# A new band build, loads of w in thirds, mixed first blocks and a SyncE store at the end of a fused convolution and maxout FFN

**Chip, cores, metric.** One core of one Trainium2 chip. The metric is the device time of one execution in microseconds (us), lower is better. Most kernels were run in several rounds beside the kernel before on the same chip. Each trace is one of those runs.

## The reference

A causal convolution with 7 softmaxed taps for each of 8 heads (24 channels each) over x of 8 x 4160 x 192, then a maxout feed-forward layer over the 33280 rows. All inputs and outputs are fp32.

```python
w = softmax(weight)                                  # 8 heads x 7 taps
y[b, s, h, :] = sum_k w[h, k] * x_pad[b, s + k, h, :]   # 6 zero rows ahead
h = max(max(y @ w1, y @ w2), y @ w3)                 # 192 -> 768
out = h @ w_out                                      # 768 -> 192
```

## The kernel before

The rows are cut into 65 blocks of 512. Each block passes through: load of x (SyncE), cast to fp16 (GpSimd), convolution as matmuls with a banded matrix of taps (`conv`, tile G), eviction to `ys`, a *repack* of `ys` into `yd` by six small DMAs (three on SyncE, three on GpSimd), a *doubling* of `yd` onto partitions 64 to 127 (one DMA on SyncE), layer 1 in six steps (`l1`, tiles lp and lq), and the second stage (`st2`, tile po). Blocks 0 and 1 are convolved in another way (`conv_dense`, tile D), with no repack. `wd` holds w1-w3 and w2-w3; `keep_warm` runs matmuls on zeros in places where TensorE would wait.

The band before: the taps are spread over 128 partitions by an fp32 matmul, softmaxed there, multiplied into seven shifted identities on VectorE and summed by seven matmuls.

```python
nc.tensor.matmul(wps, lhsT=ones[:], rhs=wk[:], start=True, stop=True)
# ... exp, sums, reciprocal, taps ...
for k in range(KW):                       # 7 products on VectorE
    nc.vector.tensor_mul(out=shifted[:, k, :, :], in0=shifted_identity_k, in1=taps_k)
keep_warm(7)
for k in range(KW):                       # 7 matmuls
    nc.tensor.matmul(ps[:], lhsT=ident16[:], rhs=shifted[:, k, :, :], start=(k == 0), stop=(k == KW - 1))
```

The order of the loads and of the first blocks, shortened:

```python
load_x(0); load_w(...)          # 6 pieces of w on SyncE and ScalarE
load_x(1); load(wos)
for t in range(2, 6): load_x(t) # x of blocks 2 to 5, all in the first burst
# ...
conv_dense(0, ...); l1(0, 0); l1(0, 1); l1(0, 2); l1(0, 3); transposes
conv_dense(1, ...); conv(2); l1(0, 4); repack(2); load_x(6); make_m(0); l1(0, 5); make_m(1)
conv(3); repack(3); double(2); load_x(7)
for t in range(1, NB):
    load_x(t + 7); cast_x(t + 5); double(t + 2)
    l1(t, 0); conv(...); repack(t + 3); st2(t - 1, ...); l1(t, 1..5)
    store(t - 1, 0, 4, (nc.gpsimd,))       # also for the last block but one
```

The softmax here doesn't subtract the row's maximum and nothing guards it: scores larger than these inputs give would overflow.

## Time and profile before

| | before |
|---|---|
| time | 482.04 us median (481.05 to 482.09, 3 runs) |
| span of the profiled core, mean granted TensorE clock | 480.0 us, 0.993 |
| TensorE busy | 468.4 us, 98% of the span |
| loop | 13.95 us for two blocks, all TensorE |

The prediction below shows the lines of this profile. One more view of it matters later: what TensorE waited for between 14 and 60 us (columns: who, for whom, us in total, times, longest). "issue" is idle time that no semaphore explains.

```profile
PE pt L284 <- DVE h L388: 1.3, 2, 1.1
PE pm L301 <- issue: 0.2, 1, 0.2
```

So from 14 us on TensorE lost 1.5 us in all. The 0.2 us of "issue" ahead of make_m (tile pm) looked like nothing.

Words used below: a DMA *lands* when its completion is signalled. A *stop* is idle time of TensorE that the profile calls "issue". A *window* is a stretch of 3.41 us: the granted clock is 1.00 or 0.50 in these traces from about 8 us on, and up to the last matmul it changed only after multiples of it (10.24 us at 1.00, then 3.41 at 0.50 before). A *pass* is one turn of the loop over t.

### The profile page before, as it was taken

The page shows a single profiled execution, that of the slowest core. Times are in us where ns is not written, and L with a number is a line of the kernel's source. Part 1 is how long each engine was busy: PE and PEld are TensorE (multiplying, and loading weights), DVE is VectorE, ACT ScalarE, POOL GpSimd, SP SyncE. Part 2 cuts the span into 40 slices and gives each one's busy share as a digit, 9 for nine tenths or more (in the row PEclk, how much of TensorE's full clock was granted, in tenths as well). Part 3 has the DMA queues.
Part 4 walks back from the last instruction along what each step waited for, and adds up shares of the span by engine and source line. Part 5 has one row for each costly group of instructions (what it writes and reads, how often), then busy time and mean ns, then how long its engine had stood idle before and what let it go on. Part 6 is the DMA issues. An engine that isn't in the chain of part 4 may idle for free.

```text
span 480.0 us, 21944 instructions
## 1 busy us (share of the span) xinstructions
PE 468.4 (98%) x9083; PEld 393.7 (82%) x9083; DVE 365.8 (76%) x609; ACT 327.1 (68%) x608; POOL 211.3 (44%) x341
## 2 busy tenths in 40 slices
PE   7899999999999999999999999999999999999994
PEld 3578888888888888888888888888888888888994
DVE  6667877778777877877787787778777777778774
ACT  5676667676666767666666766676676767667663
POOL 2654534553454355445435544543545354345210
PEclk9899999999999999999999999999999999999998
DMA  8877756665766665566666657566556666644312
GB/s 198 216 188 209 214 147 194 173 187 160 202 168 181 184 184 165 162 196 179 173 179 185 171 155 196 168 189 178 170 158 191 186 169 176 179 126 135 112 44 95
DMA packets 67603, 82.08 MB, mean 171 GB/s; under 512 B 9424, under 2 KB 55760, under 8 KB 67504
## 3 DMA queue, kind: packets, MB, share of 16 engines
q1 hardware_dynamic: 53934, 49.01, 40.6%
q0 software_dynamic: 13216, 31.38, 18.4%
q8 instruction: 71, 1.16, 1.1%
q10 hardware_dynamic: 354, 0.30, 0.2%
q14 instruction: 28, 0.23, 0.1%
HBM read 30.31 MB, written 25.56 MB: 116 GB/s over the span
## 4 chain that ended last, share of the span: by engine, by line
PE 96%; ACT 1%; DVE 1%; issue 0%; POOL 0%; POOLq 0%
PE lp L383 32%; PE po L426 30%; PE lq L383 26%; PE G L322 7%; PE D L342 1%; PE idle L196 1%; ACT r L387 0%; PE band_sum L245 0%; ACT band L268 0%; ACT w3h L262 0%; DVE h L388 0%; DVE xz L216 0%; PE pm L305 0%; PE wps L223 0%; DVE band L218 0%
## 5 line engine op out<-in xcount | busy, mean ns | idle before, releaser
L388 DVE TENSOR_TENSOR h<-r,lq 128x512 f16<-128x512 f16 x390 | 266.9, 685 | 101.8 <-ACT r L387 101.8
L387 ACT ACTIVATE r<-lp 128x512 f16<-128x512 f32 x390 | 232.7, 597 | 135.0 <-PE lp L383 89.8
L383 PE MATMUL lp<-yd,wd 64*128 64x512 f16 x1170 | 315.4, 376 | 0.1
L383 PE MATMUL lq<-yd,wd 64*128 64x512 f16 x1170 | 314.6, 375 | 0.0
L426 PE MATMUL po<-wo,h 64*128 64x192 f16 x3120 | 231.3, 243 | 0.1
L426 PEld LDWEIGHTS <-h 64*128 64x128 f16 x3120 | 186.9, 94 | 26.1 <-issue 0.3
L383 PEld LDWEIGHTS <-wd 64*128 64x128 f16 x2340 | 164.4, 94 | 20.9 <-issue 1.4
L452 POOL DMA_DIRECT2D out_dram<-o x64 | 50.7, 792 | 245.9 <-DVE o L436 229.1
L366 POOL DMA_DIRECT2D yd<-ys x189 | 95.5, 509 | 2.2 <-ACT ys L353 1.4
L426 PE MATMUL po<-m,yd 64*128 64x192 f16 x780 | 86.8, 243 | 0.0
L436 DVE TENSOR_TENSOR o<-a,po 128x384 f32<-128x384 f32 (+1 forms) x132 | 71.3, 541 | 0.6 <-ACT a L435 0.6
L146 POOL CAST x<-xf 112x960 f16<-112x960 f32 x62 | 61.6, 995 | 2.3 <-DMA xf<-in_x_dram 2.3
L435 ACT COPY a<-po 128x384 f32<-128x384 f32 (+1 forms) x132 | 61.8, 469 | 1.2 <-PE po L426 1.2
L426 PEld LDWEIGHTS <-yd 64*128 64x128 f16 x780 | 55.0, 94 | 8.1
L322 PEld LDWEIGHTS <-x 112*32 112x32 f16 x2480 | 30.0, 97 | 13.3 <-issue 13.1
L353 DVE CAST ys<-G 128x512 f16<-128x512 f32 x60 | 38.4, 681 | 0.0
L353 ACT CAST ys<-G 128x512 f16<-128x512 f32 x66 | 35.8, 589 | 2.2 <-PE G L322 0.9
L322 PE MATMUL G<-band,x 112*32 112x103 f16 (+1 forms) x2480 | 35.0, 210 | 0.0
L161 POOL CAST xz<-xf 112x240 f16<-112x240 f32 (+2 forms) x6 | 2.4, 450 | 11.3 <-DMA xf<-in_x_dram 11.3
L196 PE MATMUL idle<-idle 128*128 128x512 f16 x14 | 5.7, 546 | 1.2 <-DVE unit L212 1.2
L342 PE MATMUL D<-band,xz 112*32 112x103 f16 (+1 forms) x240 | 4.1, 240 | 1.0 <-ACT band L268 1.0
L342 PEld LDWEIGHTS <-xz 112*32 112x32 f16 x240 | 3.8, 114 | 1.5 <-issue 1.4
(50 smaller groups left out, 41.2 us busy)
## 6 DMA issues: line engine op xcount, KB each, us to landing
out_dram<-o POOLq DMA_DIRECT2D x64, 384.0 KB, 3.9
xf<-in_x_dram SPq DMA_DIRECT2D x57, 420.0 KB, 4.8
yd<-yd SPq DMA_DIRECT2D x63, 192.0 KB, 3.2
yd<-ys SPq DMA_DIRECT2D x63, 48.0 KB, 3.6
yd<-ys POOLq DMA_DIRECT2D x63, 48.0 KB, 3.3
xf<-in_x_dram SPq DMA_DIRECT2D x8, 252.0 KB, 3.1
yd<-ys SPq DMA_DIRECT2D x63, 32.0 KB, 3.2
yd<-ys POOLq DMA_DIRECT2D x63, 32.0 KB, 2.9
```

The costliest lines, as they stand in the source:

```text
L146: nc.gpsimd.tensor_copy(out=v[0:rl, q0:q1, :], in_=xf[0:rl, q0:q1, :])
L322: nc.tensor.matmul(G[i][32 * g:32 * g + 32, lo:hi], lhsT=x16[0:rlen, cb:cb + 32], rhs=band[0:rlen, h, cc:cc + hi - lo], start=True, stop=T ...
L342: nc.tensor.matmul(ps[32 * g:32 * g + 32, lo:hi], lhsT=xz[t][0:rlen, q, v, 32 * s:32 * s + 32], rhs=band[0:rlen, h, cc:cc + hi - lo], star ...
L353: copy(out=slots[t][:, i, :], in_=convs[t][i][:])
L366: (nc.sync, nc.gpsimd)[n % 2].dma_start(out=yd[r0:r0 + rows, c, :], in_=slots[t][s0:s0 + rows, half, :])
L383: nc.tensor.matmul(ps[i][:, 0:N], lhsT=wd[row, c, P * j:P * (j + 1)], rhs=y[row, c, 0:N], start=(c == 0), stop=(c == NC - 1))
L387: nc.scalar.activation(out=r[:, 0:N], in_=ps[0][:, 0:N], func=AF.Relu)
L388: nc.vector.tensor_max(out=hs[t][:, j, 0:N], in0=r[:, 0:N], in1=ps[1][:, 0:N])
L426: nc.tensor.matmul(ps[b0, i][:, s % 2, :], lhsT=a, rhs=b, start=first, stop=last)
L435: nc.scalar.copy(out=a[:, ss, :], in_=ps[s0, 0][:, ss, :])
L436: nc.vector.tensor_add(out=outs[t][:, s0:s + 1, :], in0=a[:, ss, :], in1=ps[s0, 1][:, ss, :])
L452: qs[i].dma_start(out=bass.AP(tensor=out.tensor, offset=r * D, ap=[[D, n], [step * D, s1 - s0], [1, D]]), in_=ob[p0:p0 + n, s0:s1, :])
```

## The change

The intent is to reach the loop earlier and to end sooner. The band comes from a zero-padded line of taps, of which 38 tiny matmuls each take a window. w comes in thirds on SyncE with x of block 1 between. Layer-1 steps of blocks 0 and 1 are mixed, so that TensorE has work while w and x arrive. The last block but one is stored by SyncE, so that no GpSimd store stands at the end. Cut to its core:

```diff
-    for t in range(2, 6):
+    load_x(0); load_w(0); load_w(1); load_x(1); load_w(2)
+    for t in range(2, 5):
         load_x(t)
...
-    (taps matmul, 7 products, 7 matmuls)
+    nc.vector.tensor_scalar(out=line[:, 31:31 + KW], in0=wexp[:], scalar1=wrec[:], scalar2=None, op0=mult)
+    for c in range(WIN):                                       # 38
+        nc.tensor.matmul(bps[:, c, :], lhsT=line[:, WIN - 1 - c:WIN + 31 - c],
+                         rhs=ident16[0:NHEAD, 0:NHEAD], start=True, stop=True)
+    keep_warm(6)
...
+    nc.gpsimd.dma_start(out=wo[:], in_=moe_w_out...)           # fp32 to fp16 in the DMA
+    l1(0, 0); make_wd(2, 4); transposes; l1(0, 1); l1(0, 2); l1(0, 3)
+    conv_dense(1, ...); make_wd(4, 6); l1(1, 0); l1(0, 4); transposes; l1(0, 5); l1(1, 1)
+    conv(2); l1(1, 2); repack(2); make_m(0); make_m(1); st2(0, ...); l1(1, 3); ...
+    load_x(5); double(2); load_x(6); l1(1, 4); ...; l1(1, 5)
+    conv(3); repack(3); cast_x(4); cast_x(5); cast_x(6); load_x(7); load_x(8)
...
+    convs_at = {2: (4, 5), 3: (6,)}
+    repacks_at = {2: (4,), 3: (5, 6)}
+    doubles_at = {2: (3,), 3: (4,), 4: (5, 6)}
-    for t in range(1, NB):
+    for t in range(2, NB):
         load_x(t + 7)                                          # stands ahead of double(u)
         cast_x(t + 5)
-        double(u - 1)
+        for u in doubles_at.get(t, (t + 2,)):
+            double(u)
...
-        store(t - 1, 0, 4, (nc.gpsimd,))
+        (last block but one: two halves on nc.sync; the others as before)
```

More of the change, by code (lines that the diff above doesn't have):

```diff
@@ L97 @@
     psw = ctx.enter_context(tc.tile_pool(name="psw", bufs=4, space=bass.MemoryType.PSUM))
-    NDENSE, AHEAD = 2, 3
+    NDENSE = 2
     SLOTS = ((0, 1, 2, 3), (6, 7, 4, 5))
@@ L109, with load_x @@
     x16z = const.tile([P, nlast * D + 2 * EDGE], FP16, name="x16_z")
-    def load_x(t):
+    def load_x(t, eng=nc.sync):
         if not 0 <= t < NB:
@@ L129, in load_x @@
                           ap=[[D, rlen], [step * D, k - i + 1], [1, D]])
-            nc.sync.dma_start(out=xf[0:rlen, i:k + 1, :], in_=src)
+            eng.dma_start(out=xf[0:rlen, i:k + 1, :], in_=src)
             if parts and parts[-1][0] == rlen:
@@ L156, in cast_dense @@
         for v, copy in enumerate(copies):
+            if copy is None:
+                continue
             for s in range(CYC // 32):
@@ L167, with load_w @@
     w3s = const.tile([P, NC, DFF], FP32)
-    wos = const.tile([P, NJ, D], FP32)
-    def load_w(eng, st, lo, wsrc, f0, f1):
-        eng.dma_start(out=st[lo:lo + HALF, :, f0:f1],
-                      in_=wsrc.rearrange("(c r) f -> r c f", r=HALF)[:, :, f0:f1])
-    FA = 2 * P
-    wk = const.tile([1, NHEAD * KW], FP32)
-    nc.scalar.dma_start(out=wk[:], in_=bass.AP(tensor=weight.tensor, offset=0,
-                                               ap=[[0, 1], [1, NHEAD * KW]]))
-    load_x(0)
-    load_w(nc.scalar, ws, HALF, moe_w2, 0, FA)
-    load_w(nc.sync, w3s, 0, moe_w3, 0, FA)
-    load_w(nc.sync, ws, 0, moe_w1, 0, FA)
-    load_w(nc.sync, w3s, HALF, moe_w3, FA, DFF)
-    load_w(nc.sync, ws, 0, moe_w1, FA, DFF)
-    load_w(nc.sync, ws, HALF, moe_w2, FA, DFF)
+    PW = 2 * P
+    def load_w(part):
+        f = slice(PW * part, PW * (part + 1))
+        for st, lo, wsrc in ((w3s, 0, moe_w3), (ws, 0, moe_w1), (ws, HALF, moe_w2)):
+            nc.sync.dma_start(out=st[lo:lo + HALF, :, f],
+                              in_=wsrc.rearrange("(c r) f -> r c f", r=HALF)[:, :, f])
+    wk = const.tile([NHEAD, KW], FP32)
+    nc.scalar.dma_start(out=wk[:], in_=weight)
+    load_x(0)
+    load_w(0)
+    load_w(1)
     load_x(1)
-    nc.sync.dma_start(out=wos[:], in_=moe_w_out.rearrange("(j p) c -> p j c", p=P))
-    for t in range(2, 6):
+    load_w(2)
+    for t in range(2, 5):
         load_x(t)
-    idle = const.tile([P, NBLK], FP16)
-    nc.vector.memset(idle[:], 0.0)
-    def keep_warm(n):
-        ps = psp.tile([P, NBLK], FP32, tag="p", name="idle")
-        for _ in range(n):
-            nc.tensor.matmul(ps[:], lhsT=idle[:, 0:P], rhs=idle[:], start=True, stop=True)
     ident = const.tile([P, P], FP32)
@@ L206, with keep_warm @@
         nc.gpsimd.memset(x16[:, w:w + EDGE], 0.0)
-    unit = const.tile([P, 32 + 2 * PAD], FP16)
-    nc.vector.memset(unit[:], 0.0)
-    with nc.allow_low_precision("ones and zeros"):
-        nc.vector.reduce_sum(out=unit[:, PAD:PAD + 32],
-                             in_=ident[:].rearrange("p (a c) -> p c a", c=32), axis=AXX)
+    idle = const.tile([P, NBLK], FP16)
+    nc.vector.memset(idle[:], 0.0)
+    def keep_warm(n):
+        ps = psp.tile([P, NBLK], FP32, tag="p", name="idle")
+        for _ in range(n):
+            nc.tensor.matmul(ps[:], lhsT=idle[:, 0:P], rhs=idle[:], start=True, stop=True)
+    line = const.tile([NHEAD, WIN + 31], FP16)
+    nc.vector.memset(line[:], 0.0)
     nc.vector.memset(xz[0][:], 0.0)
@@ L218 @@
     nc.vector.memset(band[:], 0.0)
-    ones = const.tile([1, P], FP32)
-    nc.vector.memset(ones[:], 1.0)
-    keep_warm(2)
-    wps = psq.tile([P, NHEAD, KW], FP32, tag="q", name="wps")
-    nc.tensor.matmul(wps[:].rearrange("p h k -> p (h k)"), lhsT=ones[:], rhs=wk[:],
-                     start=True, stop=True)
-    wexp = const.tile([P, NHEAD, KW], FP32)
-    nc.scalar.activation(out=wexp[:], in_=wps[:], func=AF.Exp)
-    wsum = const.tile([P, NHEAD], FP32)
-    nc.vector.reduce_sum(out=wsum[:], in_=wexp[:], axis=AXX)
@@ L229 @@
-    wrec = const.tile([P, NHEAD], FP32)
-    nc.vector.reciprocal(out=wrec[:], in_=wsum[:])
-    taps = const.tile([P, NHEAD, KW], FP16)
-    nc.vector.tensor_mul(out=taps[:], in0=wexp[:],
-                         in1=wrec[:].unsqueeze(2).to_broadcast([P, NHEAD, KW]))
-    shifted = const.tile([P, KW, NHEAD, WIN], FP16)
-    for k in range(KW):
-        one = unit[:, k:k + WIN]
-        nc.vector.tensor_mul(out=shifted[:, k, :, :],
-                       in0=bass.AP(tensor=one.tensor, offset=one.offset,
-                                   ap=[list(one.ap[0]), [0, NHEAD], [1, WIN]]),
-                       in1=taps[:, :, k:k + 1].to_broadcast([P, NHEAD, WIN]))
@@ L242 @@
-    keep_warm(7)
-    ps = psq.tile([P, NHEAD, WIN], FP32, tag="q", name="band_sum")
-    for k in range(KW):
-        nc.tensor.matmul(ps[:], lhsT=ident16[:], rhs=shifted[:, k, :, :],
-                         start=(k == 0), stop=(k == KW - 1))
-    keep_warm(3)
-    w3h = const.tile([P, NC, DFF], FP16)
-    parts_w3 = ((0, 0, FA), (HALF, FA, DFF))
+    keep_warm(5)
+    wexp = const.tile([NHEAD, KW], FP32)
+    wsum = const.tile([NHEAD, 1], FP32)
+    nc.scalar.activation(out=wexp[:], in_=wk[:], func=AF.Exp, accum_out=wsum[:])
@@ new lines @@
+    wrec = const.tile([NHEAD, 1], FP32)
+    nc.vector.reciprocal(out=wrec[:], in_=wsum[:])
+    nc.vector.tensor_scalar(out=line[:, 31:31 + KW], in0=wexp[:], scalar1=wrec[:], scalar2=None,
+                            op0=mybir.AluOpType.mult)
+    bps = psq.tile([32, WIN, NHEAD], FP32, tag="q", name="band_cols")
+    for c in range(WIN):
+        nc.tensor.matmul(bps[:, c, :], lhsT=line[:, WIN - 1 - c:WIN + 31 - c],
+                         rhs=ident16[0:NHEAD, 0:NHEAD], start=True, stop=True)
@@ L250 @@
+    keep_warm(6)
+    for a in range(4):
+        nc.scalar.copy(out=band[32 * a:32 * a + 32, :, 32 * a:32 * a + WIN],
+                       in_=bps[:].rearrange("p c h -> p h c"))
+    cast_dense(0, (nc.vector.tensor_copy, nc.vector.tensor_copy))
+    w3h = const.tile([HALF, NC, DFF], FP16)
     wd = const.tile([P, NC, DFF], FP16)
+    w3t = const.tile([P, NJ, D], FP16)
+    wo = const.tile([P, NJ, D], FP16)
+    m16 = const.tile([P, 2, D], FP16)
     def make_wd(j0, j1):
@@ L256, in copy_w3, with cast_w3 @@
     def copy_w3(copy, part):
-        lo, f0, f1 = part
-        copy(out=w3s[HALF - lo:P - lo, :, f0:f1], in_=w3s[lo:lo + HALF, :, f0:f1])
-    def cast_w3(copy, part):
-        lo, f0, f1 = part
-        copy(out=w3h[lo:lo + HALF, :, f0:f1], in_=w3s[lo:lo + HALF, :, f0:f1])
-    cast_dense(0, (nc.scalar.copy, nc.scalar.copy))
-    copy_w3(nc.scalar.copy, parts_w3[0])
-    make_wd(0, 1)
-    for a in range(4):
-        nc.scalar.copy(out=band[32 * a:32 * a + 32, :, 32 * a:32 * a + WIN], in_=ps[32 * a:32 * a + 32, :, :])
-    copy_w3(nc.vector.tensor_copy, parts_w3[1])
-    cast_w3(nc.scalar.copy, parts_w3[0])
-    w3t = const.tile([P, NJ, D], FP16)
-    wo = const.tile([P, NJ, D], FP16)
-    m16 = const.tile([P, 2, D], FP16)
+        f = slice(PW * part, PW * (part + 1))
+        copy(out=w3s[HALF:P, :, f], in_=w3s[0:HALF, :, f])
+    def cast_w3(part):
+        f = slice(PW * part, PW * (part + 1))
+        nc.gpsimd.tensor_copy(out=w3h[:, :, f], in_=w3s[0:HALF, :, f])
     def transpose_w3(g):
-        ps = psq.tile([P, 2, D], FP32, tag="q", name=f"pt{g}")
+        ps = psw.tile([P, 2, D], FP32, tag="w", name=f"pt{g}")
         for k in range(2):
@@ L282, in transpose_w3 @@
             for c in range(NC):
-                row = slice(0, HALF) if g == 0 else slice(HALF, P)
-                nc.tensor.matmul(ps[:, k, HALF * c:HALF * (c + 1)], lhsT=w3h[row, c, js],
-                                 rhs=ident16[row, row], start=True, stop=True)
-        copy = nc.scalar.copy if g == 1 else nc.vector.tensor_copy
-        copy(out=w3t[:, 2 * g:2 * g + 2, :], in_=ps[:])
-    cast_dense(1, (nc.gpsimd.tensor_copy, nc.gpsimd.tensor_copy))
-    nc.gpsimd.tensor_copy(out=wo[:], in_=wos[:])
-    cast_x(2)
-    cast_x(3)
-    cast_x(4)
-    cast_x(5)
+                nc.tensor.matmul(ps[:, k, HALF * c:HALF * (c + 1)], lhsT=w3h[:, c, js],
+                                 rhs=ident16[0:HALF, 0:HALF], start=True, stop=True)
+        nc.scalar.copy(out=w3t[:, 2 * g:2 * g + 2, :], in_=ps[:])
     def make_m(i):
@@ L405, in st2 @@
                         mm.append((y[row, 2, tok], m16[row, 1, :]))
-                    mm += [(hT[row, j, P * s:P * (s + 1)], wo[row, j, :]) for j in range(NJ)]
+                    hh = [(hT[row, j, P * s:P * (s + 1)], wo[row, j, :]) for j in range(NJ)]
+                    mm = hh + mm if t == 0 else mm + hh
                     todo[i] += [(s, n == 0, n == len(mm) - 1, m) for n, m in enumerate(mm)]
@@ L459, in begin @@
         outs[t] = outp.tile([P, 4, D], FP32, tag="o", name=f"o_{t}")
-    conv_dense(0, (nc.scalar, nc.vector, nc.scalar))
-    make_wd(1, 2)
+    begin(0)
+    begin(1)
+    copy_w3(nc.vector.tensor_copy, 0)
+    make_wd(0, 2)
+    conv_dense(0, (nc.scalar, nc.scalar, nc.scalar))
+    copy_w3(nc.vector.tensor_copy, 1)
+    cast_w3(0)
+    cast_w3(1)
+    cast_dense(1, (nc.gpsimd.tensor_copy, None))
+    nc.gpsimd.dma_start(out=wo[:], in_=moe_w_out.rearrange("(j p) c -> p j c", p=P))
+    cast_w3(2)
+    cast_x(2)
+    l1(0, 0)
     make_wd(2, 4)
-    begin(0)
-    l1(0, 0)
+    transpose_w3(0)
     l1(0, 1)
-    keep_warm(2)
-    make_wd(4, NJ)
-    cast_w3(nc.scalar.copy, parts_w3[1])
+    transpose_w3(1)
+    cast_dense(1, (None, nc.scalar.copy))
     l1(0, 2)
+    copy_w3(nc.scalar.copy, 2)
     l1(0, 3)
-    for g in range(NJ // 2):
-        transpose_w3(g)
     conv_dense(1, (nc.scalar, nc.vector, nc.scalar))
+    make_wd(4, 6)
+    l1(1, 0)
+    l1(0, 4)
+    transpose_w3(2)
+    l1(0, 5)
+    l1(1, 1)
     conv(2)
     evac(2, 0)
-    l1(0, 4)
+    l1(1, 2)
     evac(2, 1)
     repack(2)
+    cast_x(3)
+    make_m(0)
+    make_m(1)
+    st2(0, 0, NJ)
+    l1(1, 3)
+    st2(0, 1, NJ)
+    load_x(5)
+    double(2)
     load_x(6)
-    make_m(0)
-    l1(0, 5)
-    make_m(1)
-    conv(3)
+    l1(1, 4)
+    st2(0, 2, NJ)
+    l1(1, 5)
+    conv(3, ((psp, "p"), (psq, "q")))
     evac(3, 0)
@@ L488 @@
     repack(3)
-    double(2)
+    cast_x(4)
+    cast_x(5)
+    cast_x(6)
     load_x(7)
-    for t in range(1, NB):
-        u = t + AHEAD
+    load_x(8)
+    for u in range(3, NJ):
+        st2(0, u, NJ)
+    store(0, 0, 4, (nc.gpsimd,))
+    convs_at = {2: (4, 5), 3: (6,)}
+    repacks_at = {2: (4,), 3: (5, 6)}
+    doubles_at = {2: (3,), 3: (4,), 4: (5, 6)}
+    for t in range(2, NB):
         load_x(t + 7)
         cast_x(t + 5)
-        double(u - 1)
+        for u in doubles_at.get(t, (t + 2,)):
+            double(u)
         begin(t)
         l1(t, 0)
-        if t == 1:
-            conv(u)
+        us = convs_at.get(t, (t + 3, t + 4) if t % 2 == 0 else ())
+        for n, u in enumerate(us):
+            conv(u, (((psw, "w"), (psw, "w")), ((psp, "p"), (psq, "q")))[n])
+        for u in us:
             evac(u, 0)
-            evac(u, 1)
-        elif t % 2 == 0:
-            conv(u)
-            conv(u + 1, ((psp, "p"), (psq, "q")))
-            evac(u, 0)
-            evac(u + 1, 0)
-            evac(u + 1, 1, nc.vector.tensor_copy)
+        for u in us[::-1]:
             evac(u, 1, nc.vector.tensor_copy)
-        repack(u)
+        for u in repacks_at.get(t, (t + 3,)):
+            repack(u)
         st2(t - 1, 0, NJ)
@@ L515 @@
             st2(t - 1, j, NJ)
-        store(t - 1, 0, 4, (nc.gpsimd,))
+            if t == NB - 1 and j == 3:
+                store(t - 1, 0, 2, (nc.sync,))
+        if t == NB - 1:
+            store(t - 1, 2, 4, (nc.sync,))
+        else:
+            store(t - 1, 0, 4, (nc.gpsimd,))
     for u in range(NJ):
```

## The prediction

> **What bounds the kernel now.** I read the page first, then the chain of waits, then the stretches of two microseconds at the start, then the first 30 us and the last 7 us in order of time.
>
> ```profile
> span 480.0 us, 21944 instructions
> PE 468.4 (98%) x9083; PEld 393.7 (82%) x9083; DVE 365.8 (76%) x609; ACT 327.1 (68%) x608; POOL 211.3 (44%) x341
> PE   7899999999999999999999999999999999999994
> ```
>
> TensorE is busy from about 26 us to 474 us without a gap. In the chain, the convolution that opens every second block (G, L322) starts at 34.04 and again at 47.99: 13.95 us for two blocks, all of it TensorE. The diff leaves that loop's instructions and order alone from its second or third pass on. So the change can only move three things: when the loop is reached, how many TensorE instructions are still owed then, and what follows the last matmul.
>
> The start, by the windows of the TensorE clock (columns: window, length, TensorE busy and its instructions, granted clock, DMA share, GB/s):
>
> ```profile
> 9.01:12.42 3.41, 2.37 (x126) 1.00 1.04 227
> 12.42:15.83 3.41, 3.29 (x23) 1.00 1.11 272
> 15.83:19.24 3.41, 1.94 (x55) 1.00 1.10 275
> 19.24:22.65 3.41, 3.41 (x152) 0.50 0.69 182
> ```
>
> The third window is only 1.94/3.41 = 57% busy, and the fourth runs at half clock; there the dense convolution of block 1 takes 2.52 us where that of block 0 took 1.55. Before 9 us the page says 1.00, but seven idle matmuls took 3.10 us of the chain, 0.44 each, where a 512-column pair of layer 1 takes 0.21 in the loop: the array was at half clock there too.
>
> What releases the first dense convolution, in order of time:
>
> ```profile
> 5.16 2.79 DVE L237 TENSOR_TENSOR shifted<-unit,taps 128x304 f16<-128x304 f16 x7
> 7.03 1.98 PE L245 MATMUL band_sum<-shifted,ident 128*128 128x304 f16 x7
> 9.05 1.65 ACT L268 CAST band<-band_sum 32x304 f16<-32x304 f32 x4 [0.82 <-PE band_sum L245]
> 10.75 1.55 PE L342 MATMUL D<-band,xz 112*32 112x103 f16 x120 [1.04 <-ACT band L268]
> ```
>
> And how block 2 reaches layer 1 (repack of ys into yd, then the copy yd to yd that doubles it), on the SyncE queue:
>
> ```profile
> 22.85 2.01 SPq L366 DMA_DIRECT2D yd<-ys  x3
> 24.91 1.06 SPq L130 DMA_DIRECT2D xf<-in_x_dram  x1
> 26.78 1.78 SPq L366 DMA_DIRECT2D yd<-ys  x3
> 28.81 0.52 SPq L372 DMA_DIRECT2D yd<-yd  x1
> ```
>
> The doubling (3.4 us to landing) ends at 32.2, and block 2's first layer-1 matmul starts at 33.13: hidden, by 0.9 us.
>
> The end (all instructions of the closing line):
>
> ```profile
> L542 SPq EVENT_SEMAPHORE  x11: 17/28/28, 475.6 to 479.9; - x11
> L542 POOLq DRAIN  x3: 40/102/6327, 472.9 to 479.7; - x3
> L542 SPq DRAIN  x3: 7/7/13, 477.9 to 479.5; - x3
> ```
>
> SyncE has seen the last store land and drains at 477.97. GpSimd's drain starts at 472.88, just before its last store is issued (472.90), and lasts 6.33 us, to 479.21. It is the last to arrive, by 1.24 us, though its store landed at 475.8.
>
> [...] the six 64-column transposes took 0.33 us with 0.19 for the last, (0.33-0.19)/5 = 28 ns[...]. [...] the trace moves 227 to 275 GB/s with two queues in use. [...] here a last store takes 2.4 and the doubling 3.4, and I use those. [...]
>
> **The change part by part.**
>
> *Band.* Removed: the fp32 tap matmul, the reductions and seven products on VectorE (2.79 us) and seven band matmuls (1.98). Now the softmax is done on 8 partitions straight from the loaded weights: the table load ends about 2.6 (no second DMA issue on ScalarE), weights land at about 3.0 (first x part: 2.4 us to landing), Exp, reciprocal and product 0.2 us each, so the line is ready at 3.6. 38 tiny matmuls of 8 columns at half clock, estimate 2 x 28 ns = 56 ns: 2.2 us, to 5.9. The four band copies, 1.65 us as today, end at 7.7 if the strided PSUM read costs nothing. But six idle matmuls of 0.43 stand between on TensorE: 5.9 + 2.6 = 8.4. The dense convolution starts at 8.4 instead of 10.75.
>
> *Layer 1 of block 0.* Partly cold, the convolution ends near 10.2; three evictions of 0.58, all on ScalarE now, end at 11.0; l1(0,0) is done at 11.3 and its ReLU starts there, where today the first starts at 13.39. Lead: 2.0 us.
>
> *Weights in thirds.* Cumulated bytes over the same rate, plus 1.9 us to landing (today: the first 1.02 MB are moved at about 6.1 and landed at 8.1): second third at 10.5, x1 at 12.4, last third at 14.9. None of these is what the first matmul waits for. But VectorE takes the wd of the second third after h(0,0): 12.65 + 0.96 = 13.6, which holds l1(0,2). ScalarE must then do r(0,2), a w3 copy of 0.83 and r(0,3) before it evicts block 1: 16.4, 17.0, 17.6. VectorE evicts its third, then makes the last wd (0.96): 18.8, which holds l1(0,4).
>
> *Mixing.* From there each layer-1 step waits for the PSUM pair two before (ReLU 0.60, max 0.69): l1(0,5) 19.8, l1(1,1) 20.8, conv(2) 21.4 to 22.0. Today conv(2) ends at 22.28. The lead in starting has become work done: four more layer-1 steps, 4 x 0.64 = 2.6 us, are behind TensorE. Block 2's second eviction ends at 23.9 (today 24.33).
>
> *Block 2.* GpSimd issues its last repack 0.55 later, 3.0 to landing, 0.1 for the wait, 3.4 for the doubling: 23.9 + 7.1 = 31.0. Today SyncE stood at block 3's repack and lost about half a microsecond there. TensorE is through with all it may do (make_m, l1(1,3..5), conv(3), st2(0)) at about 29.2. So it waits 1.8 us, and block 2 starts at 31.0 instead of 33.13, with conv(4), 0.52 us, still owed. Gain at the start: 33.13 - 31.0 - 0.52 = 1.6 us.
>
> *End.* The last block but one is stored by SyncE in halves, the second issued at about 472.7, before 473.49 when SyncE issues its next. GpSimd's last store is then one block earlier and its drain over by 473. The end moves to SyncE's 477.97: gain 1.2 us.
>
> *Sum.* 1.6 + 1.2 = 2.8 us if the clock holds. For it not holding I take off 0.5 (below): 482.04 - 2.3 = 479.7 us.
>
> **The rivals.** (a) *TensorE bound throughout:* the doubling lands in time, block 2 starts at 29.2, start gain 3.4, time about 477.4. For it: the order was evidently made to fill TensorE. Against: 7.1 us of eviction, repack and doubling that today's trace shows link by link. (b) *Clock:* between 16 and 20 us my schedule has TensorE about half busy, as in today's throttled window; and the wait of 1.8 us at 29 to 31 leaves 1.6/3.41 = 47% of a window if it falls in one. The first costs about 1.2 us of conv(2), the second about 3.4/2 = 1.7. Each maybe one in three, not both in full: about 0.5 net, since today pays one such window as well, mostly hidden in waits. If both bite, the start gain is gone: 481 to 482. (c) *Band slower than today's path:* tiny matmuls at 100 ns or strided reads at twice the time. Either adds up to 1.6 us at the front, but the idle matmuls and the later waits for wd hide part; time about 480.5. (d) *Drain not caused by the store:* then the end gains nothing: 480.9.
>
> **Range and chances.** The end's 1.2 us is nearly certain; the start spans -1 to +3.4. I set 477.8 to 481.7. A gain over 2% needs 9.6 us, more than all the TensorE idle of the start that waits could give back; a loss over 2% needs a fault in the loop. 0.01 each.
>
> **What would show it.** Dense convolution starting at 8 to 9 us. The first ReLU near 11.3. Waits of TensorE for VectorE's wd near 13 and 18. A TensorE gap ahead of block 2 ended by the doubling, near 31. Loop still 13.95 us per two blocks. GpSimd's long drain over before SyncE's, about 1.3 us between SyncE's drain and the end gone. Wrong if conv(2) comes before 20.5 or after 23, if the gap ahead of block 2 is missing, if half-clock windows appear after 29 us, or if the loop's period changes.

What is marked as cut there held general statements on the hardware, and no term of the sum: that stays 1.6 + 1.2 - 0.5 = 2.3 us, 482.04 - 2.3 = 479.7. The 0.5 for the clock is the author's estimate from the windows shown (57% busy, then a granted clock of 0.50). That w in thirds moves at the same rate as before was the author's estimate too.

## The result

| | before | after |
|---|---|---|
| time, first measurement | 481.94 us median (481.05 to 482.09, 4 runs) | 486.10 us median (485.56 to 487.08, 4 runs) |
| ratio after/before, 95% interval | | 1.0092 (1.0072 to 1.0113) |
| time, second measurement, on a later occasion | 483.53 us (481.77 to 486.23, 11 runs) | 484.99 us (482.34 to 487.89, 6 runs) |
| ratio after/before, 95% interval | | 1.0028 (0.9988 to 1.0068) |

A ratio is the mean time of one kernel's fast runs over the mean of the other's in the same rounds, so it is not quite the ratio of the medians. The kernel is slower where I had predicted faster, by 0.9% in the first measurement and by 0.3% (interval over 1) in the second. All ten runs lie above the top of my range, 481.7. It stays within 2%.

The page of the changed kernel, answering to the three lines of before:

```profile
span 484.1 us, 21993 instructions
PE 468.2 (97%) x9109; PEld 390.8 (81%) x9109; DVE 364.3 (75%) x603; ACT 324.9 (67%) x606; POOL 212.4 (44%) x340
PE   8687999999999999999999999999999999999996
```

TensorE has the same work (468.2 us) in a longer span; the second to fourth of the forty slices (12 to 48 us) read 6, 8, 7 where before has 8, 9, 9. The start in order of time, the lines that answer to the band's:

```profile
3.73 1.17 PE L226 MATMUL band_cols<-ident,line 8*32 8x8 f16 x38 [0.22 <-DVE line L222]
4.93 1.64 ACT L230 CAST band<-band_cols 32x304 f16<-32x304 f32 x4 [1.93 <-PE band_cols L226]
7.50 1.70 PE L309 MATMUL D<-band,xz 112*32 112x103 f16 x120
10.37 0.60 ACT L354 ACTIVATE r<-lp 128x512 f16<-128x512 f32 x1 [0.46 <-PE lq L350]
```

The start works: the dense convolution is at 7.50 instead of 10.75, the first ReLU at 10.37 instead of 13.39. Then what TensorE waited for between 14 and 60 us:

```profile
PE lq L350 <- DMA yd<-yd: 5.1, 2, 3.4
PE lp L350 <- issue: 1.9, 1, 1.9
```

Two waits for a doubling (yd to yd), 1.65 us at block 2 and 3.44 at block 3, and 1.85 us of "issue". In order of time, the "issue" is this hole in layer 1 of block 1, between two matmuls of one accumulation; no semaphore stands there, ScalarE is idle too, and VectorE is but for 0.43 us:

```profile
20.01 0.37 PE L350 MATMUL lq<-yd,wd 64*128 64x512 f16 x1 [0.28 <-DVE h L355]
22.24 0.37 PE L350 MATMUL lp<-yd,wd 64*128 64x512 f16 x1 [1.85 <-issue]
```

The SyncE queue, which answers to the queue lines of before; at 29.58 it issues block 2's doubling, at 36.70 block 3's:

```profile
29.58 0.52 SPq L339 DMA_DIRECT2D yd<-yd  x1
30.20 1.68 SPq L130 DMA_DIRECT2D xf<-in_x_dram  x1
31.98 1.79 SPq L333 DMA_DIRECT2D yd<-ys  x3
33.81 2.15 SPq L130 DMA_DIRECT2D xf<-in_x_dram  x4
36.70 0.52 SPq L339 DMA_DIRECT2D yd<-yd  x1
```

Four load instructions for x of three blocks (7, 8, 9; 1.26 MB, at 420 KB each) stand between block 3's repack and its doubling. The doubling lands on its last DMA engine at 44.24, 7.54 us after its issue at 36.70; the page's median for these copies is 3.2. Then the clock (columns as in the prediction's windows):

```profile
41.99:45.40 3.41, 1.11 (x37) 0.58 (x41) 0.04 (x1) 0.44 (x1) 3.41 (x6) 1.00 1.06 322
45.40:48.81 3.41, 3.41 (x54) 2.25 (x42) 1.43 (x3) 1.34 (x3) 1.68 (x4) 0.50 0.55 150
```

(Here the busy times of all engines are listed: TensorE, its weight loads, VectorE, ScalarE, GpSimd; then clock, DMA share, GB/s.) The window at 41.99 is 1.11/3.41 = 33% busy and the next runs at half clock (0.50), which by my estimate costs 3.41/2 = 1.7 us. The half-clock window of before at 19.24 is not there. Last, the end (all instructions of the closing line):

```profile
L544 POOLq DRAIN  x3: 46/102/6570, 472.1 to 483.8; - x3
L544 SPq DRAIN  x3: 7/7/7, 483.2 to 483.5; - x3
```

GpSimd's long drain still takes 6.57 us, but it starts at 472.1, a block before the end, and is over at 478.7, before SyncE's at 483.2. From the end of the last matmul to the end of the span it is 4.7 us now (479.4 to 484.1), and 6.2 before (473.8 to 480.0).

A ledger of the start, from the first dense convolution to the convolution that opens the pass t = 4, from where on both kernels have the same 13.95 us loop:

| us | before | after |
|---|---|---|
| first dense convolution | 10.75 | 7.50 |
| opening convolution of pass 4 | 47.92 | 53.78 |
| between them, TensorE busy | 35.33 | 36.50 |
| between them, TensorE idle | 1.84 | 9.78 |

So a lead of 3.25 us is followed by 7.94 us more of idle and 1.17 us more of busy time (part of it block 6's convolution, done one pass earlier, worth 0.52 in the loop): 7.94 + 1.17 - 3.25 = 5.86 us later.

### The profile page after: what moved, and what is told of

It is laid out like the page before. It is cut to its first block, busy times and chain, and to the rows that moved or that the text cites. A ratio compares the mean times of both kernels' runs of the same rounds, so it can differ in the third digit from the quotient of the medians.

```text
span 484.1 us, 21993 instructions
## 1 busy us (share of the span) xinstructions
PE 468.2 (97%) x9109; PEld 390.8 (81%) x9109; DVE 364.3 (75%) x603; ACT 324.9 (67%) x606; POOL 212.4 (44%) x340
## 3 DMA queue, kind: packets, MB, share of 16 engines
q8 instruction: 71, 1.16, 1.1%
## 4 chain that ended last, share of the span: by engine, by line
PE 93%; DMA 2%; DVE 1%; ACT 1%; issue 1%; SPq 1%; ACTq 0%; DVEq 0%
PE lp L350 31%; PE po L394 29%; PE lq L350 25%; PE G L289 6%; DMA yd<-yd 2%; DMA yd<-ys 1%; PE idle L205 1%; PE D L309 0%; DVE wd L244 0%; SPq L130 0%; ACT yd L315 0%; DVE h L355 0%; ACT L219 0%; ACT r L354 0%; PE band_cols L226 0%
## 5 line engine op out<-in xcount | busy, mean ns | idle before, releaser
L252 POOL CAST w3h<-w3s 64x768 f16<-64x768 f32 x3 | 2.5, 825 | 4.0 <-DMA w3s<-in_moe_w_dram 4.0
L315 ACT CAST yd<-D 128x512 f16<-128x512 f32 x5 | 2.7, 589 | 1.8 <-PE D L309 1.8
```

## The experiments

**What the stop is.** I counted TensorE's records in order of start. In the page's list of DMA queues there are two called "instruction"; one has 71 packets and 1.16 MB: 16 KB each, and 2 x 9109 matmuls and weight loads over 71 packets make 257 instructions for each (an estimate, from the page's two counts). The stop is at record 705 in the changed kernel, and, as the runs below showed, at record 705 in others too, whatever stands there (a direct count of the kept traces puts 702 or 703 records ahead of it; the name 705 is kept):

```
kernel            what is record 705   stop (us)             2nd instruction packet   landed -> going on
before            make_m               0.2, to 23.39         20.87 + 1.16             1.4
e1_tail_only      make_m               21.59 -> 23.93 (2.34) 21.27 + 1.17             1.5
e4_band_only      conv of block 3      20.95 -> 26.20 (5.26) 23.73 + 1.11             1.4
after             layer 1 of block 1   20.39 -> 22.24 (1.85) 19.82 + 1.08             1.3
e2_double_first   layer 1 of block 1   20.41 -> 22.55 (2.13) 20.02 + 1.07             1.5
e3_warm_wait      layer 1 of block 1   21.45 -> 21.96 (0.52) 19.66 + 0.99             1.3
e9_extra_load     make_m               22.28 -> 25.62 (3.35) 23.09 + 1.19             1.3
e8_band_late      conv of block 3      20.89 -> 22.38 (1.49) 20.00 + 0.93             1.5
e7_late_loads     layer 1 of block 1   none                  17.50 + 0.94             -
```

TensorE goes on 1.3 to 1.5 us after the second packet of this queue has landed. I read this as TensorE having run out of instructions; no record shows it directly.

All fourteen kept traces have this timing. From 6 us on they have 22 idle stretches of TensorE over 0.15 us that no semaphore explains, and every one ended 1.2 to 1.6 us after such a packet had landed. At record 449, 256 before 705, TensorE stopped for 0.25 us in the changed kernel (0.51 in its second trace), 0.94 in run 2, 1.41 in run 8 and 1.19, 0.22 and 0.36 in runs 9 to 11, each time until 1.3 to 1.6 us after the first packet.

**Run 1, the tail alone.** The kernel before with one edit:

```diff
-        store(t - 1, 0, 4, (nc.gpsimd,))
+            if t == NB - 1 and j == 3: store(t - 1, 0, 2, (nc.sync,))
+        if t == NB - 1: store(t - 1, 2, 4, (nc.sync,))
+        else: store(t - 1, 0, 4, (nc.gpsimd,))
```

> The kernel before with one part of the change alone: the store of the last block but one goes over SyncE instead of GpSimd; nothing else. Theory: GpSimd's drain of 6.3 us follows its own last store, so that drain then starts a block earlier and its end no longer sets the end of the program; expected 1.2 to 1.5 us less than the kernel before (480.4 to 480.8 us where that one takes 482.0), the last TensorE instruction at the same time within 0.3 us. Rival: the drain is the closing line's own and comes whatever was stored, so the time stays at 482.0 and GpSimd still arrives last.

481.41 us (480.47 to 482.92), ratio 0.9975 (0.9956 to 0.9994): 1.2 us gained.

```profile
L547 POOLq DRAIN  x3: 40/102/6245, 468.2 to 479.8; - x3
L547 SPq DRAIN  x3: 7/7/7, 479.2 to 479.6; - x3
```

The long drain moved with GpSimd's last store, to 468.2, and no longer sets the end; the tail after the last matmul is 4.65 us. The theory holds. What it did not expect: in this trace the last matmul came 1.6 us later than before, because the stop at record 705 was 2.34 us long and a half-clock window followed. Up to there this kernel is the kernel before, whose own trace had a stop of 0.2 us: its packet came at nearly the same time (20.87 against 21.27), but it had a half-clock window ahead of the stop (19.24 to 22.65 at 0.50; a convolution of 120 matmuls took 2.52 us there, 1.55 at full clock) and came to record 705 at 23.2 instead of 21.6. The length of the stop therefore varies between executions of the same code.

**Run 2, block 3's doubling ahead of two loads.** The changed kernel with:

```diff
-    load_x(7)
-    load_x(8)
+    load_x(7)
...
-        load_x(t + 7)
+        if t != 2: load_x(t + 7)
...  (after double(3))
+        if t == 2: load_x(8); load_x(9)
```

> The changed kernel with the loads of blocks 8 and 9 moved behind the doubling copy of block 3 on the SyncE queue, no other edit. Theory: the doubling of block 3 took 7.54 us to land because three loads of x were issued just ahead of it; with two of them behind it, it should land in 3.5 to 4.5 us, block 3's first layer-1 matmul start at 41 to 41.5 instead of 44.3, the half-clock window after it vanish, and the whole take 481.0 to 482.5 us (about 4 to 5 less than 486.1). A wait of 0.5 to 1 us may come up at block 4. Rival: the doubling was slow for another reason (GpSimd's part of the repack, one slow DMA engine), so the wait of about 3.4 us stays and the time is 485.5 to 486.5.

483.67 us (482.13 to 485.18), ratio 1.0020 (0.9997 to 1.0044).

```profile
PE lq L350 <- DMA yd<-yd: 3.8, 3, 1.6
PE lp L350 <- issue: 2.1, 1, 2.1
```

The doubling was issued at 37.58 and TensorE went on at 42.69, at most 5.1 us later instead of 7.5. The wait at block 3 shrank to 1.61 us, no half-clock window came after it, and a wait of 0.96 us came up at block 4. The direction is right and the size is not: I expected 481.0 to 482.5. Its ratio lies clear of the changed kernel's first (1.0092), but not of the second (1.0028), so its worth in time is not settled; the shorter wait is what the trace shows. The load of block 7 was still ahead, and the stop at record 705 was untouched.

**Run 3, the array kept busy in the wait.** The changed kernel with 15 idle matmuls ahead of block 3's first layer-1 step:

```diff
+        if t == 3:
+            keep_warm(15)
```

> The changed kernel with 15 idle matmuls put ahead of block 3's first layer-1 matmul, in the place where TensorE waits 3.4 us for the doubling; no wait is removed. Theory: the wait costs twice, once itself and once by the half-clock window that comes after it (45.4 to 48.8); with the array busy during the wait that window is gone and the kernel is 1.5 to 1.9 us faster than the changed one: 484.2 to 484.6. Rival: the half-clock window would have come anyway or its work was hidden, so the time is 485.9 to 486.4; worse if the idle matmuls outlast the wait.

486.31 us (483.69 to 487.59), ratio 1.0080 (1.0063 to 1.0097). The trace is of the 483.69 us run, the fastest of six:

```profile
40.00:43.50 3.50, 3.50 (x24) 1.53 (x18) 1.31 (x3) 0.87 (x2) 1.52 (x2) 1.00 0.93 231
43.50:47.00 3.50, 3.50 (x79) 2.13 (x80) 1.42 (x3) 1.73 (x3) 2.50 (x6) 1.00 0.74 206
```

There the wait is filled and the clock stays full; that run's mean clock is 1.000. Its stop was also only 0.52 us, so its time is not the filled wait's alone. The other five took 485.80 to 487.59 at mean clocks of 0.991 to 0.996. One half-clock window is 1.7/480 = 0.0036 of the mean, and half clock after the last matmul can take as much again (0.0035 in the trace of before), so by this estimate the three at 0.991 to 0.995 had at least one window, somewhere that no trace shows; of the two at 0.996 it can't be told. The median did not move and lies in the rival's range. The run shows the effect once; as a measure of its worth it is inconclusive.

**Run 4, the band alone.** The kernel before with the new band build and its keep-warm counts, nothing else (order of loads and blocks as before):

```diff
-    keep_warm(2); (taps matmul, 7 products); keep_warm(7); (7 matmuls); keep_warm(3)
+    keep_warm(5); (line of taps); (38 tiny matmuls); keep_warm(6)
```

> The kernel before with one part of the change alone: the band from a zero-padded line of taps and 38 tiny matmuls, with the keep-warm matmuls fitted to it. Theory: the dense convolution of block 0 then starts about 3 us earlier (7.5 instead of 10.75), but the loads of w and x that follow arrive when they did, so the array waits for those instead and the whole gains 0 to 1 us: 481.0 to 482.0. Rival A: the band was the head of the critical path all the way, so the whole gains about 3 us: 479. Rival B: the new band takes away warm work and an added idle window puts a later stretch at half clock, so that it is 0.5 to 1.5 us slower.

485.61 us (484.74 to 489.45), ratio 1.0070 (1.0042 to 1.0097): 3 us slower by the medians. None of the three expectations had that size or its cause.

```profile
PE G L303 <- issue: 5.3, 1, 5.3
```

The stop sits in a convolution, which has nothing in common with the layer-1 step of the changed kernel except its place in the stream. Its packet came at 23.73, when the burst of loads (235 GB/s at 21 to 22 us, 49 at 23 to 24) had drained. Two half-clock windows followed, from 25.6 to 32.5. The trace is of the slowest of the six runs (489.45 us; the others took 484.74 to 486.31), so its stop of 5.26 us is probably longer than in the others.

**Run 5, later loads.** The changed kernel; x of blocks 3 and 4 is loaded once VectorE has made the last third of wd. A one-element memset of the target tile makes the load wait (in the trace both were issued at 18.40):

```diff
-    for t in range(2, 5):
-        load_x(t)
+    load_x(2)
...
     make_wd(4, 6)
+    load_x(3, gate=nc.vector)     # gate: nc.vector.memset(xf[0:1, 0, 0:1], 0.0) ahead of the DMA
+    load_x(4)
```

> The changed kernel with the loads of blocks 3 and 4 held back until VectorE has made the last third of wd (about 17.7 us) instead of standing in the burst of loads at the start; no other edit. In six traces so far TensorE stopped at its instruction 705, whatever stood there (make_m, a convolution, layer 1), and went on 1.3 to 1.5 us after the second 16 KB packet of the instruction queue had landed; that packet came when the burst of loads drained (19.8 us here, 20.9 before, 23.7 in the run with the new band alone). Theory: the packet waits behind the burst; with 840 KB less in it, it should come at 16 to 17.5 us, the stop at instruction 705 (1.85 us, at 20.39) shrink below 0.3 us, and the kernel gain 1 to 2 us: 484.2 to 485.2. The wait at block 3 is untouched and stays. Rival: the packet's time has nothing to do with the loads (it follows a fixed time after the request), so the stop stays near 1.85 us and the time at 486.

483.06 us (482.57 to 484.77), ratio 1.0002 (0.9977 to 1.0027).

```profile
PE lq L351 <- DMA yd<-yd: 1.7, 1, 1.7
PE G L290 <- POOL x L148: 1.5, 2, 1.2
```

The packet came at 17.50 instead of 19.82 and the stop is gone: no "issue" is left in this list. So is the wait at block 2. In their place block 3's convolution waits 1.2 us for its later x, and 1.7 us remain at block 3. The rival, that the packet's time has nothing to do with the loads, falls. Against the first measurement the gain is 3.0 us by the medians and 0.9%, or 4.3 us, by the ratios, larger than I expected; against the second (1.0028) the intervals overlap. One half-clock window is left (33.05 to 36.46).

**Run 6, the band with later loads.** As run 4, with x of blocks 4 and 5 loaded after block 1's dense convolution:

```diff
-    for t in range(2, 6):
+    for t in range(2, 4):
         load_x(t)
...
     conv_dense(1, ...)
+    load_x(4, gate=nc.vector); load_x(5)
...
-    cast_x(4); cast_x(5)            # before the blocks
     repack(2)
+    cast_x(4); cast_x(5)
```

> The kernel before with the new band alone, as in the run that became 3 us slower with a 5.26 us stop of TensorE at instruction 705, but with the loads of blocks 4 and 5 held back until the dense convolution of block 1 is evacuated (about 20.5 us). Theory: that loss was the instruction packet waiting behind the burst, so the stop falls below 1 us and the kernel with the new band alone is as fast as the kernel before or up to 2 us faster: 480.5 to 482.5, against 485.6. Rival: the loss came from the band itself (other clock windows, a later wd), so it stays at 484.5 to 486.

483.56 us (482.67 to 484.44), ratio 1.0005 (0.9982 to 1.0029), against 1.0070 without the edit; these intervals do not overlap.

```profile
PE G L303 <- issue: 1.5, 1, 1.5
```

The time came to where the theory had it (as fast as before); the stop fell from 5.26 to 1.49 us, less far than the 1 us that I had written. Since run 4's trace was its slowest run, the ratios carry this comparison and not the two stops. The band's loss was the instruction packet and the half-clock windows behind its stop, not the band.

**Run 7, a longer burst.** The kernel before with two more loads of 420 KB that nothing reads, at the end of the burst:

```diff
     for t in range(2, 6):
         load_x(t)
+    for k in range(2):
+        extra = const.tile([112, NQ, D], FP32, name=f"extra_{k}")
+        nc.sync.dma_start(out=extra[:], in_=(560 rows of x))
```

> The kernel before with two more loads of 420 KB of x appended to the burst at the start, into tiles that nothing reads. Theory: the burst ends some 3 us later (estimate: 840 KB at the 280 GB/s that the windows show at 14 to 21 us), the second instruction packet moves from 20.9 to 23.5 to 24.5 us, TensorE stops at instruction 705 for 2.5 to 3.5 us instead of 0.2, and the kernel takes 2.5 to 4 us longer: 484.5 to 486.5. Rival: the packet does not wait behind loads; it stays at about 21 us, and the kernel loses 0 to 1 us at most through the later repack of block 2.

486.46 us (486.00 to 487.38), ratio 1.0067 (1.0043 to 1.0092): 3.2 us slower by the ratio.

```profile
25.63 1.14 PE L305 MATMUL pm<-wo,w3t 128*128 128x192 f16 x6 [3.35 <-issue]
```

The packet moved from 20.87 to 23.09, a little less than I wrote, and the stop grew from 0.2 to 3.35 us. Run 1's trace, which has the same start without the extra bytes, already had a stop of 2.34 us, so the stop's growth in a single trace proves little. What the bytes moved is the packet, by 1.8 us against run 1 and 2.2 against before, and the times of all six runs, each above the slowest of before's eleven (485.64). Two windows of half clock followed (before has one).

**Run 8, both edits.** The changed kernel with the edits of runs 2 and 5.

> The changed kernel with both edits that helped alone: loads of blocks 3 and 4 held back (alone: ratio to the kernel before 1.0002 instead of 1.0092), and the doubling of block 3 ahead of the loads of blocks 8 and 9 (alone: 1.002). Theory: the two losses are different ones and add up; neither the stop at instruction 705 nor a wait above 0.3 us at block 3 is left, and the ratio to the kernel before is 0.993 to 0.997. Rival, which the first candidate suggests: the loads of blocks 8 and 9 now stand ahead of block 4's repack and doubling, so a wait of 1 to 3 us comes up at block 4, with a half-clock window after it where it is long enough, and the ratio stays at 0.998 to 1.003.

482.45 us (481.38 to 483.25), ratio 0.9976 (0.9947 to 1.0005).

```profile
PE D L310 <- issue: 1.4, 1, 1.4
PE lq L351 <- DMA yd<-ys: 1.1, 1, 1.1
PE lq L351 <- DMA yd<-yd: 0.8, 1, 0.8
```

Neither the stop at record 705 nor a wait at block 3 is left (its doubling landed in 3.47 us), and the ratio is 0.5 to 1.2% below the changed kernel's two, though its interval overlaps the second's. But the first line is the stop at record 449: 1.41 us, where run 5 with the same loads held back had none. And 0.8 us at block 4 and 1.1 at block 5 came up, as the rival said. Moving loads behind one doubling puts them ahead of the next.

**Runs 9 to 11, candidates.** The first adds to run 5's edit an earlier convolution of blocks 2 and 3 and an earlier doubling of both. The second puts the repacks and doublings of blocks 3 to 6 ahead of loads and casts; the third turns the SyncE queue once more. Each against the one before it (the first against run 5):

```diff
first:
-    l1(0, 4); transposes; l1(0, 5); l1(1, 1); conv(2)
+    l1(0, 4); transposes; conv(2); l1(0, 5); repack(2); cast_x(3); load_x(5); l1(1, 1)
-    load_x(5); double(2); load_x(6); l1(1, 4); ...; conv(3); repack(3); load_x(7); load_x(8)
+    double(2); load_x(6); st2(0, 0); conv(3); l1(1, 3); repack(3); load_x(7); double(3); ...; load_x(8)
second:
-    make_wd(4, 6); load_x(3, gate=nc.vector); load_x(4)
+    cast_x(2); load_x(3, gate=nc.gpsimd); load_x(4)
-    load_x(7); double(3); ...; load_x(8)
+    double(3); load_x(7)
-    pass 2: load_x(9); cast_x(7); repack(4)  | pass 3: load_x(10); cast_x(8); double(4); repack(5); repack(6)
+    pass 2: repack(4); repack(5); load_x(8); cast_x(7)  | pass 3: double(4); double(5); repack(6); load_x(9); cast_x(8)
third:
     double(2)
-    load_x(6)
     conv(3); repack(3)
+    load_x(6)
     double(3); load_x(7)
-    pass 2: repack(4); repack(5); load_x(8)  | pass 3: double(4); double(5); repack(6); load_x(9)
+    pass 2: repack(4); load_x(8); double(4); repack(5); load_x(9)  | pass 3: repack(6); double(5); load_x(10)
```

> A candidate to beat both: the changed kernel with the loads of blocks 3 and 4 held back as in the run of that name, the convolution of block 2 right after the last transposes (its x is cast by 18.6), the convolution of block 3 ahead of the rest of block 0's second stage, the doubling of block 3 ahead of the loads of blocks 8 and 9, and the doubling of block 2 straight after its repack. Theory: with the stop at instruction 705, the waits at blocks 2 and 3 (1.65 and 3.44 us) and the half-clock window after them (1.7 us) gone, some 7 to 8.5 us go from 486.1: 477.5 to 479. Rival: new waits take the place of some (a doubling behind a load, an instruction packet later on), and it ends at 480 to 482.

482.47 us (480.90 to 484.00), ratio 0.9980 (0.9954 to 1.0006): the rival. Pass 2 began at 30.7 instead of 33.7, and then block 4 waited 2.80 us for its doubling, with a half-clock window after it (48.59 to 52.00; the trace is of the slowest of the six runs):

```profile
PE lq L351 <- DMA yd<-yd: 3.4, 2, 2.8
```

> The first candidate once more, with every repack and doubling of blocks 3 to 6 ahead of the loads of x on the SyncE queue: block 7's load behind the doubling of block 3, block 8's behind the repacks of blocks 4 and 5, blocks 9 to 11 one place later than they were, the casts behind the repacks on GpSimd, and the two held-back loads released by GpSimd's cast of block 2. Theory: the first candidate lost 2.8 us waiting for block 4's doubling and 1.7 us in the half-clock window after it; both go, nothing longer than 0.6 us is waited for after block 2, and the ratio to the kernel before is 0.987 to 0.992 (476 to 479 us where that one takes 482.5). Rival: another doubling or load comes late (block 5 or 6, or x of blocks 9 and 10), and the ratio is 0.994 to 0.999.

480.89 us (478.79 to 481.56), ratio 0.9936 (0.9906 to 0.9965). Faster, though less than the theory's 0.987 to 0.992: block 4 still waited 1.50 us.

> The second candidate with one more turn of the SyncE queue: the load of block 6 behind the repack of block 3, the doubling of block 4 ahead of the repack of block 5, the loads of blocks 9 to 11 behind the doublings. Theory: the second candidate still waited 1.50 us for block 4's doubling, which was issued at 43.15 behind two repacks and a load; issued before 40 us it lands in time, the loop runs from block 2 on without a wait over 0.6 us, and the ratio to the kernel before falls from 0.9936 to 0.989 to 0.992. Rival: the waits that are left are set by how much the DMA engines carry in this stretch, not by the order, so a wait of 1 us or more comes up at another block and the ratio stays at 0.993 to 0.996.

478.38 us (477.70 to 480.14), ratio 0.9895 (0.9861 to 0.9929), as the theory had it.

```profile
span 477.1 us, 21994 instructions
PE 467.0 (98%) x9109; PEld 391.0 (82%) x9109; DVE 364.8 (76%) x603; ACT 324.9 (68%) x606; POOL 212.6 (45%) x341
PE   8799999999999999999999999999999999999995
```

From 26 us to pass 4 (46.24) TensorE is busy without a hole: 20.24 of 20.24 us. Block 4's doubling was issued at 42.60, later than the 40 I had written, and landed in time all the same. On one chip and in the same rounds this version takes 478.38, the kernel before 483.53 and the changed one 484.99.

**Run 12, the changed kernel again**, on that chip, for a second trace.

> The changed kernel once more, unedited, on the same chip and beside the same runs of the kernel before as the third candidate: a second trace of it, to see which of its losses come again. Expected if the four losses are its own: a stop at instruction 705 of 0.5 to 2.5 us, a wait of 1 to 2 us at block 2 and of 2.5 to 3.5 us at block 3, and a ratio of 1.007 to 1.011. If the wait at block 3 was the accident of one execution it would be gone, and the ratio at 1.003 or less.

484.99 us (482.34 to 487.89), ratio 1.0028 (0.9988 to 1.0068); the trace is of a 483.40 us run.

```profile
PE lq L350 <- DMA yd<-yd: 3.5, 2, 2.2
PE lp L350 <- issue: 2.1, 1, 2.1
```

The stop (2.11 us, at the same record) and the waits at blocks 2 and 3 (1.30 and 2.18) come again, all three. The wait at block 3 is 1.3 us shorter and no half-clock window follows it, so 1.3 + 1.7 = 3.0 us of the first trace's loss are missing in this one. The three waits came in both traces and in run 2's; how long block 3's is, and with it whether the clock falls, differs between executions. The two traced spans differ by 2.5 us (484.1 and 481.6); that the same causes the rest of the spread of 5.5 us is not shown. The ratio missed the band that I had written, on the side of less loss.

## Why the prediction was wrong

I predicted 479.7 us and a gain, and got 486.1 and then 485.0 us and a loss. Step by step:

- **Band: right, under-rated.** 8.4 was expected for the dense convolution, 7.50 came. The 38 matmuls took 1.17 us, 31 ns each, where I had doubled 28 ns to 56 for a half clock. (My 5.9 + 2.6 is 8.5, a slip of 0.1.) The strided read of PSUM cost nothing: four copies in 1.64 us, 0.41 each, and 1.65 before.
- **Layer 1 of block 0: right, under-rated.** First ReLU at 10.37 against 11.3; a lead of 3.0 us instead of 2.0.
- **Weights in thirds: right.** VectorE's wd held TensorE to 12.61 and 17.79, where I had 13.6 and 18.8.
- **Mixing: this step failed first.** I had conv(2) at 21.4, it came at 22.78, although everything ahead of it ran a microsecond early; without the stop of 1.85 us it would have been at 20.9. I took TensorE to be limited by semaphores and PSUM alone. A second supply, its own instructions, comes by DMA as well: 71 packets of 16 KB in the page's list. In the loop this hardly shows: the fourteen traces have five later stops of this kind, of 0.25 to 0.63 us. In the start it does: at record 705 the stop was 0.2 to 5.3 us, where there was one. Runs 5, 6 and 7 show the cause: with fewer bytes in the burst the packet came earlier (17.50 instead of 19.82, 20.00 instead of 23.73) and the loss went or shrank, with more bytes it came later (23.09 instead of 20.87) and the loss grew.
- **Block 2: mechanism right, shifted.** The wait was 1.65 us against 1.8, but block 2 started at 32.97 instead of 31.0, because the stop had delayed its convolution; its eviction ended at 25.28 instead of 23.9, and the rest of the chain took 7.7 us instead of 7.1.
- **The loop: this step failed hardest.** "The diff leaves that loop's instructions and order alone from its second or third pass on" left out the passes before: the diff rewrites passes 2 to 4. I followed block 2's doubling link by link and never followed block 3's, whose doubling stands behind three loads in the changed queue. It took 7.54 us to land and cost TensorE 3.44 us (6.81 and 2.18 in the second trace). Run 2 shrank the wait by moving two of the loads; in runs 8 and 9, with fewer loads ahead of it, the doubling landed in 3.47 us, and runs 8 to 11 have no wait above 0.6 us at block 3.
- **Clock: my rival (b), in another place.** I had a half-clock window at 16 to 20 or behind a wait at 29 to 31 us, and gave 0.5 us for it. It came at 45.4, behind block 3's wait, for 1.7 us. In the traces, every stop or wait of TensorE of 2.3 us or more was followed by one (the first trace, runs 1, 4, 7 and 9), and stops of up to 2.2 us mostly were not. My reading that a window 57% busy is followed by half clock was too simple. From 8 to 70 us of the fourteen traces, the five full-clock windows that were at most 41% busy were all followed by half clock (0, 19, 33, 35 and 41% in runs 4 and 9, the changed kernel, runs 1 and 7). Above that the busy share alone does not decide: windows that were 57% busy were followed by half clock (1.94 of 3.41 us before, 1.95 in run 5, where no single wait was over 1.2 us), while less busy ones kept the full clock (1.87 of 3.41 at 11.28 in the changed kernel, 1.68 at 39.88 in run 5, 1.81 at 11.75 in run 8). Of the signs of being wrong that I had written down, this one alone came true, a half-clock window after 29 us: conv(2) at 22.78, the gap ahead of block 2 and the loop's period stayed within what I had allowed.
- **End: right.** 1.2 us expected; 1.5 us in the changed kernel's trace, 1.2 us in run 1's time. GpSimd's long drain took 6.33 us before, 6.57 in the changed kernel and 6.25 in run 1, each time from its last store on.

The sum: 1.85 + 3.44 + 1.7 = 7.0 us; 0.5 of it, for the clock, was in my 479.7, so 6.5 were not, which makes 486.2 where 486.1 was measured. That this fits so closely is partly luck: the sizes are those of one trace, and in the second trace the same terms add up to 2.11 + 2.18 + 0 = 4.3 us. Of the rivals none had the cause: (c) and (d) are refuted, (a) did not happen, since block 2's wait came, and (b) had one of three terms.

What stays open: why the packet comes later with a longer burst was not taken apart. The traces don't show when it was asked for or where it waited. The start of the kernel before has two traces (its own and run 1's) whose stops differ by 2.1 us, and most other kernels have one, so how each of the terms varies from execution to execution is not known. And the worth of a filled wait (run 3) was seen in one execution of six.

## What to carry to other kernels

When a change makes the start denser, look at which DMAs are in flight when TensorE's next instruction packet is due (the stops here were at records 449 and 705), and hold back loads that nothing needs soon: here 840 KB more or less of early x was worth about 3 us (runs 6 and 7). In a queue that carries both prefetches and links of a chain, follow every block through it until the order is the steady one, not only the first; here three prefetches ahead of one doubling cost 3.44 us (2.18 in the second trace). A stop of "issue" without a semaphore deserves a count of instructions before a story: the one of 0.2 us in the kernel before was the warning.
